# q and k laid out head dimension first by the host: attention and two expert layers on one Trainium2 core

## The chip, the cores and the metric

The kernel runs on one core of one Trainium2 chip. The metric is the device time of one launch in microseconds (us); the host's part, which lays out the inputs, is not in it. Everything is computed in fp32 up to the second expert layer, which multiplies fp16 halves of split fp32 values. In the profile PE is TensorE (PEld its weight loads), DVE VectorE, ACT ScalarE, POOL GpSimd and SP SyncE, whose queue issues the DMAs.

## What is computed

```python
# q, k, v: (4, 8, 576, 64) = batch, heads, tokens, head dimension
scores = (1 / 8) * q @ k.T + slope[h] * -|i - j|      # ALiBi
scores = where(0 <= i - j < 128, scores, -1e9)        # causal window of 128
attn   = exp(scores - max) / (sum + 1e-9)
x      = (attn @ v) as (2304, 512)                    # tokens x heads*dim
# first expert layer, soft: 8 experts of 4 slots
logits = x @ phi                                      # (2304, 32)
slots  = softmax over tokens(logits).T @ x            # (32, 512)
out_s  = relu(slots_e @ w1[e]) @ w2[e]                # per expert
x      = softmax over slots(logits) @ out_s
# second expert layer, dense: gate by 8 Sinkhorn rounds, P (2304, 8)
out    = sum over e of P[:, e] * (relu(x @ m1[e]) @ m2[e])   # 512 -> 1024 -> 512
```

## The kernel before

Attention works on 18 tiles of 128 rows. A tile t is one chunk c (64 tokens, nine of them) of the two images j of a pair; partitions 0 to 63 belong to one image and 64 to 127 to the other. A tile is done in two steps (s = 2t and 2t + 1) of four head pairs' halves: two pairs g, each with heads a = 0, 1. The loop over s at lines 475 to 526 is the order of work on every engine, written by hand; the instructions of an engine run in that order.

- `load_nat` (127) loads q and k by tokens, 64 tokens x 8 heads x 64 values in one DMA, in runs of 256 bytes; `load_v` (137) loads v by tokens, again in runs of 256 bytes.
- `emit_tr` (147) turns q and k on PE, so that the head dimension lies on the partitions (two heads on 128), and copies them from PSUM to `qT` and into the ring `kT` of four slots; slots 0 and 1 have second images behind the ring (line 158), so that three chunks are always adjacent.
- `emit_qk` (169) makes the scores of a step: 8 products of 64 x 64 with up to 192 columns, each in one quarter of PE's array.
- `emit_sm` (188) adds the bias from `rel_sb` and takes the negated maximum on DVE; `emit_exp` (209) makes the exponentials on ACT, with their sum as accumulator output; `emit_nm` (216) divides by that sum on DVE.
- `emit_pt` (224) turns the weights on PE (up to six 128 x 128 transposes a step), and ACT copies them to `ptt`.
- `emit_pv` (237) multiplies: v is the stationary operand (`lhsT`), the weights move (`rhs`), and the result has the head dimension on the partitions: head a gives the output half, image j the tile `xp[j]`. From the third chunk on 8 products have 128 rows and 8 have 64 (`steps`, 251 and 253); in the first chunk all 8 have 64, in the second all 8 have 128.
- `emit_xt` (268) copies that to `xT` (head dimension on partitions), and `emit_x` (273) turns it into `xn` (tokens on partitions). Every four tiles `group` (343) and at the end `group_end` (379) do the softmax over tokens and collect the slots' inputs; both need `xT` and `xn`.

All three PSUM pools are small: three buffers for the scores (`ps_s`), three for everything that is turned (`ps_t`), one for the products with v (`ps_x`). SP issues all loads in program order; at most eight are on their way, since each waits for the one eight before it. Beside q, k and v it loads a quarter of an expert's w1 in each step from s = 2 on (`pre`), w2 of expert 0 at s = 26 and 30, then, where attention's pools have been, w2 of experts 1 to 3. The first expert layer (`mm1`, 780) starts with w1 of expert 0; m2 and m1 of the second layer's first expert go over w1 of experts 0 and 1 once these are used (`order`, 734). The second expert layer (from 888) is a long row of fp16 products with three parts per operand pair.

Of the kernel before, what the change touches and what calls it, by code (L numbers as in the profile page):

```python
# [20 lines left out]
NPRE = 8  # L21


@with_exitstack
def tile_kernel(ctx: ExitStack, tc: tile.TileContext, q, k, v, phi, w1, w2, w_gate, m1, m2, rel, out):
    nc = tc.nc
    B, H, S, D = q.shape
    N, DM = out.shape
    E, _, F = w1.shape
    NS = phi.shape[1]  # L30
# [26 lines left out]
    def load_part(nm, e, pool, part, nparts):  # L57
        if part == 0 and pool is not None:
            wt[nm, e] = pool.tile([128, 4096], F32, tag="w", name="w")
        t = wt[nm, e]  # L60
        src = {"w1": w1, "w2": w2, "m1": m1, "m2": m2}[nm][e].rearrange("(c p) f -> p c f", p=128)
        n = src.shape[1]
        n0, n1 = n * part // nparts, n * (part + 1) // nparts
        nc.sync.dma_start(out=t.rearrange("p (c f) -> p c f", c=n)[:, n0:n1, :], in_=src[:, n0:n1, :])
# [30 lines left out]
    with tc.manual_schedule():  # L95
        with ExitStack() as ab:
# [5 lines left out]
            with ExitStack() as at:  # L102
                nat = at.enter_context(tc.tile_pool(name="nat", bufs=2))
                one = at.enter_context(tc.tile_pool(name="a1", bufs=1))
                ep = at.enter_context(tc.tile_pool(name="ep", bufs=3))
# [7 lines left out]

                kT = one.tile([128, 4, 2, 6 * CH], F32, name="kT")
# [3 lines left out]

                rel_sb = one.tile([128, 2, 4, 192], F32, name="rel_sb")


                qT = one.tile([128, 4, 2, 64], F32, name="qT")

                natt = {}
                vt = {}

                def load_nat(t):
                    bp, c = divmod(t, NCH)
                    for nm, src in (("k", k), ("q", q)):
                        nt_ = nat.tile([128, H, D], F32, tag=nm + "n", name=nm + "n")  # L130
                        for j in range(2):
                            nc.sync.dma_start(
                                out=nt_[CH * j:CH * j + CH],
                                in_=src[2 * bp + j, :, CH * c:CH * c + CH, :].rearrange("h i d -> i h d"))
                        natt[nm, t] = nt_

                def load_v(bp, c, j=None):


                    j = c % 2 if j is None else j  # L140
                    t = vp.tile([128, H, D], F32, tag="v%d" % j, name="v")
                    r0, r1 = 64 if c < 0 else 0, 64 if c == NCH - 1 else 128
                    s0 = max(CH * c, 0)
                    nc.sync.dma_start(out=t[r0:r1], in_=v[2 * bp + j].rearrange("h s d -> s h d")[s0:s0 + r1 - r0])
                    vt[bp, c, j] = t

                def emit_tr(t, nm, gs=range(4)):
                    src = natt[nm, t]
                    ps = ps_t.tile([128, 4, 128], F32, tag="pt", name="pt")
                    for i, g in enumerate(gs):  # L150
                        nc.tensor.transpose(
                            ps[:, i, :], src[:, 2 * g:2 * g + 2, :].rearrange("p a d -> p (a d)"), idn)
                    pv_ = ps[:, 0:len(gs), :].rearrange("p g (j i) -> p g j i", j=2)
                    if nm == "k":
                        sl_ = t % 4
                        nc.vector.tensor_copy(out=kT[:, :, :, CH * sl_:CH * sl_ + CH], in_=pv_)
                        if sl_ < 2 and t >= 4:
                            nc.scalar.copy(out=kT[:, :, :, CH * (sl_ + 4):CH * (sl_ + 5)], in_=pv_)
                    else:
                        nc.vector.tensor_copy(out=qT[:, gs[0]:gs[-1] + 1], in_=pv_)  # L160
# [8 lines left out]
                def emit_qk(s):  # L169
                    t, hf = divmod(s, 2)  # L170
                    c = t % NCH
                    nch = min(c, 2) + 1
                    k0 = CH * ((t - nch + 1) % 4)
                    k1 = k0 + CH * nch
                    col = 192 - (k1 - k0)

                    ps = [ps_s.tile([128, 2, 256], F32, tag="s", name="s") for _ in range(2)]
                    for gg in range(2):
                        g = 2 * hf + gg
                        for j in range(2):  # L180
                            for a in range(2):
                                r0, c0 = CH * (a ^ j), CH * a
                                nc.tensor.matmul(ps[j][c0:c0 + CH, gg, col:192], lhsT=qT[r0:r0 + CH, g, j, :],
                                                 rhs=kT[r0:r0 + CH, g, j, k0:k1], start=True, stop=True,
                                                 tile_position=(r0, c0))
                    sc[s] = (ps, col)

                def emit_sm(s):
# [6 lines left out]
                    sm = sp.tile([128, 4], F32, tag="sm", name="sm")  # L195
                    c = (s // 2) % NCH
                    for hh in range(4):
# [7 lines left out]
                            in1=rel_sb[:, j, 2 * hf + gg, col:192], scale=-0.125, scalar=3e38,  # L205
                            op0=ALU.add, op1=ALU.min, accum_out=mx[:, hh:hh + 1])
                    et[s] = (e_t, runs, sm, mx)

                def emit_exp(s):
                    _, runs, sm, mx = et[s]  # L210
                    for hh in range(4):
                        nc.scalar.activation(  # L212
                            out=runs[hh], in_=runs[hh], func=AF.Exp,
                            bias=mx[:, hh:hh + 1], scale=-1.0, accum_out=sm[:, hh:hh + 1])

                def emit_nm(s):
                    _, runs, sm, _ = et[s]
                    rc = sp.tile([128, 4], F32, tag="rc", name="rc")
                    nc.vector.tensor_scalar_add(rc, sm, 1e-9)
                    nc.vector.reciprocal(rc, rc)  # L220
                    for hh in range(4):
                        nc.vector.tensor_scalar_mul(runs[hh], runs[hh], rc[:, hh:hh + 1])

                def emit_pt(s):
                    c = (s // 2) % NCH
                    e_t, _, _, _ = et.pop(s)
# [10 lines left out]
                def emit_pv(s):  # L237
# [3 lines left out]
                    if hf == 0:  # L241
                        xps[t] = [ps_x.tile([128, 4, 64], F32, tag="xp%d" % j, name="xp") for j in range(2)]
                    xp = xps[t]
# [11 lines left out]

                    for i0 in range(0, len(steps), 2):
                        for gg in range(2):
                            g = 2 * hf + gg
                            for i in (i0, i0 + 1):
                                j, vc, r0, r1, blk = steps[i]  # L260
                                for a in range(2):
                                    o = 128 * blk + 64 * (a ^ j)
                                    nc.tensor.matmul(
                                        xp[j][64 * a:64 * a + 64, g, :],
                                        lhsT=vt[bp, vc, j][r0:r1, 2 * g + a, :], rhs=ptt[r0:r1, gg, o:o + 64],
                                        start=(i < 2 and gg == 0), stop=(i >= len(steps) - 2), skip_group_check=True)

                def emit_xt(t):
                    xT[t] = sp.tile([128, DC, 128], F32, tag="xT", name="xT", bufs=4)
                    for j, xp in enumerate(xps.pop(t)):  # L270
                        nc.vector.tensor_copy(out=xT[t][:, :, 64 * j:64 * j + 64], in_=xp)

                def emit_x(t):
                    ps = ps_t.tile([128, 4, 128], F32, tag="pt", name="pt")
                    for cc in range(DC):
                        nc.tensor.transpose(ps[:, cc, :], xT[t][:, cc, :], idn)
                    xn[t] = sp.tile([128, DM], F32, tag="xn", name="xn", bufs=4)
# [977 lines left out]
```

## Time and profile before

| | us |
|---|---|
| median of 3 runs | 965.99 (965.25 to 966.2) |
| profiled execution: span from first to last instruction | 962.0 |
| what lies around the span, by the median run | 4.0 |
| PE busy | 928.2 (96%) |
| DVE busy | 737.5 (77%) |
| ACT busy | 612.5 (64%) |
| POOL busy | 542.1 (56%) |

The shares are means over stages with different limits. Attention runs up to about 152 us, the first expert layer to 205, the second fills the rest. The page's slices of 24 us show a DMA share of 80% and more up to about 190 us and of 60% to 216, then little; of 94,659 DMA packets 63,696 are smaller than 512 bytes. PE and PEld overlap: a product's weights are loaded while others run, and products in different parts of the array overlap, so that an operation's mean duration times its count can be far above its busy time. Each fp32 product shows as two records, a transpose as one.

### The profile page before, as it was taken

What the parts mean: (1) busy time and instruction counts of PE and PEld (TensorE: products, weight loads), DVE (VectorE), ACT (ScalarE), POOL (GpSimd) and SP (SyncE); (2) the same over time, 40 slices, a digit from 0 to 9 for tenths busy, and PEclk for the clock granted to TensorE, in tenths of its full rate; (3) what the DMA queues carried; (4) which work ended last, traced back from release to release, by engine and by line L of the source; (5) the groups of instructions that cost most, each with busy time, mean ns of one, the idle gap of its engine ahead of it and who ended that gap; (6) DMA issues with size and microseconds to landing.
All of it is one profiled execution on the core that took longest, in us unless ns stands there. A gap on an engine that the chain in (4) does not pass through costs nothing.

```text
span 962.0 us, 24533 instructions
## 1 busy us (share of the span) xinstructions
PE 928.2 (96%) x9629; PEld 781.6 (81%) x9629; DVE 737.5 (77%) x1919; ACT 612.5 (64%) x1494; POOL 542.1 (56%) x624
## 2 busy tenths in 40 slices
PE   8898899889999999999999999999999999999997
PEld 5666675357888888888888888888888888888886
DVE  6888896666988777787778777877777778777775
ACT  5777784746767777666657664766576656764442
POOL 1000001213788479848974986589658956985442
PEclk9999999999999999999999999999999999999999
DMA  8999999960200500040022002200220020001222
GB/s 175 250 239 236 264 292 322 383 227 2 99 2 2 171 17 2 31 158 1 2 86 102 1 1 91 98 1 2 94 95 1 2 97 4 1 2 34 56 48 64
DMA packets 94659, 90.20 MB, mean 94 GB/s; under 512 B 63696, under 2 KB 67792, under 8 KB 94544
## 3 DMA queue, kind: packets, MB, share of 16 engines
q1 hardware_dynamic: 94544, 88.64, 32.0%
q8 instruction: 75, 1.23, 0.5%
q14 instruction: 40, 0.33, 0.1%
HBM read 82.07 MB, written 4.72 MB: 90 GB/s over the span
## 4 chain that ended last, share of the span: by engine, by line
PE 74%; DVE 2%; ACT 1%; issue 0%; DVEq 0%
PE x L1053 38%; PE y L1053 28%; PE z L979 6%; PE m L681 1%; DVE ops L992 0%; DVE s L1004 0%; PE m L556 0%; DVE acc L1065 0%; DVE prob L948 0%; ACT acc L1063 0%; ACT ops L989 0%; DVE rs L936 0%; ACT r L1000 0%; PE m L942 0%; ACT t L564 0%
## 5 line engine op out<-in xcount | busy, mean ns | idle before, releaser
L1053 PEld LDWEIGHTS <-ops 128*128 128x128 f16 x6048 | 592.2, 98 | 75.1 <-issue 5.0
L1011 POOL TENSOR_TENSOR ops<-s,ops 128x512 f16<-128x512 f32 x287 | 332.0, 1159 | 224.1 <-ACT ops L1008 223.7
L1053 PE MATMUL x<-w2h,ops 128*128 128x256 f16 x2304 | 413.8, 273 | 3.3 <-ACT acc L1063 2.7
L1053 PE MATMUL y<-w2h,ops 128*128 128x256 f16 x1728 | 319.0, 273 | 0.3 <-POOL ops L1011 0.2
L1053 PE MATMUL x<-w2l,ops 128*128 128x256 f16 x1152 | 314.1, 273 | 0.0
L1008 ACT CAST ops<-s 128x512 f16<-128x512 f32 x288 | 177.5, 617 | 212.7 <-DVE s L1004 210.3
L1053 PE MATMUL y<-w2l,ops 128*128 128x256 f16 x864 | 235.5, 273 | 0.0
L1067 DVE SCALAR_TENSOR_TENSOR acc<-x,pe,acc 128x256 f32<-128x256 f32 x252 | 121.7, 483 | 76.9 <-PE x L1053 75.5
L989 ACT ACTIVATE ops<-z 128x512 f16<-128x512 f32 x216 | 128.6, 595 | 35.1 <-PE z L979 33.4
L992 DVE SCALAR_TENSOR_TENSOR ops<-z,ops 128x512 f16<-128x512 f32 x216 | 146.9, 680 | 0.0
L1067 DVE SCALAR_TENSOR_TENSOR acc<-y,pe,acc 128x256 f32<-128x256 f32 x189 | 91.2, 483 | 58.5 <-PE y L1053 58.1
L639 POOL TENSOR_TENSOR w2l<-w,w2h 128x256 f16<-128x256 f32 x168 | 112.4, 673 | 0.0
L1004 DVE SCALAR_TENSOR_TENSOR s<-z,r 128x512 f32<-128x512 f32 x144 | 98.2, 682 | 12.0 <-ACT r L1000 6.0
L1004 DVE SCALAR_TENSOR_TENSOR s<-z,s 128x512 f32<-128x512 f32 x144 | 98.2, 682 | 6.3 <-ACT ops L989 5.3
L979 PE MATMUL z<-ct,stk 128*128 128x256 f16 x576 | 86.5, 273 | 1.4 <-ACT stk L724 0.7
L774 POOL MEMSET hz<- 128x480 f32 x2 | 1.0, 498 | 140.5 <-ACT fo L313 139.2
L642 ACT CAST w2h<-w 128x256 f16<-128x256 f32 x168 | 67.5, 402 | 0.4 <-POOL w L639 0.4
L979 PEld LDWEIGHTS <-stk 128*128 128x128 f16 x576 | 55.6, 98 | 10.8 <-issue 2.6
L212 ACT ACTIVATE et<-et,mx 128x192 f32<-128x192 f32 (+2 forms) x144 | 61.2, 430 | 3.6 <-DVE mx L203 3.6
L234 ACT COPY ptt<-pt 128x384 f32<-128x384 f32 (+2 forms) x72 | 30.1, 444 | 19.6 <-PE pt L233 19.3
L1000 ACT ACTIVATE r<-z 128x512 f32<-128x512 f32 x72 | 42.4, 589 | 0.0
L639 POOL TENSOR_TENSOR w<-w 128x256 f32<-128x256 f32 x56 | 41.0, 733 | 0.0
(192 smaller groups left out, 898.4 us busy)
## 6 DMA issues: line engine op xcount, KB each, us to landing
w<-in_moe_w_dram SPq DMA_DIRECT2D x68, 512.0 KB, 7.0
w<-in_moe_w_dram SPq DMA_DIRECT2D x14, 2048.0 KB, 8.3
kn<-in_k_dram SPq DMA_DIRECT2D x36, 128.0 KB, 5.6
qn<-in_q_dram SPq DMA_DIRECT2D x36, 128.0 KB, 5.5
v<-in_v_dram SPq DMA_DIRECT2D x18, 256.0 KB, 6.2
out_dram<-acc SPq DMA_DIRECT2D x34, 128.0 KB, 2.4
w<-in_moe_w_dram SPq DMA_DIRECT2D x2, 1024.0 KB, 6.9
stk<-sh SPq DMA_DIRECT2D x56, 16.0 KB, 1.8
```

The lines of the kernel that those rows point to most:

```text
L212: nc.scalar.activation(out=runs[hh], in_=runs[hh], func=AF.Exp, bias=mx[:, hh:hh + 1], scale=-1.0, accum_out=sm[:, hh:hh + 1])
L639: nc.gpsimd.tensor_tensor(out=out_, in0=x_, in1=y_, op=ALU.subtract)
L642: nc.scalar.copy(out=hi[:, i, r], in_=src[:, r])
L979: nc.tensor.matmul(ps[:, i], lhsT=stk[e][:, 128 * ft:128 * ft + 128], rhs=ct.rearrange("p (a n) t -> p a n t", a=2)[:, :, n, :], start=Tru ...
L989: nc.scalar.activation(out=ops_[m][:, k_, 0], in_=zb(m, i, j), func=AF.Relu)
L992: nc.vector.scalar_tensor_tensor(out=ops_[m][:, k_, 1], in0=zb(m, i, j), scalar=0.0, in1=ops_[m][:, k_, 0], op0=ALU.max, op1=ALU.subtract)
L1000: nc.scalar.activation(out=new_sum(m, "r21"), in_=zb(m, 2, 1), func=AF.Relu)
L1004: nc.vector.scalar_tensor_tensor(out=new_sum(m, nm), in0=zb(m, i, j), scalar=0.0, in1=o, op0=ALU.max, op1=op)
L1008: nc.scalar.copy(out=ops_[m][:, k_, 0], in_=sm_[m, nm])
L1011: eng.tensor_tensor(out=ops_[m][:, k_, 1], in0=sm_[m, nm], in1=ops_[m][:, k_, 0], op=ALU.subtract)
L1053: nc.tensor.matmul(out_, lhsT=a_[:, k_, l_, i, :], rhs=r_[:, k_, i, :], start=(first and j == 0), stop=(j == len(todo) - 1 and 1 in parts) ...
L1067: nc.vector.scalar_tensor_tensor(out=o, in0=ps, scalar=pe_[e][:, t:t + 1], in1=o, op0=ALU.mult, op1=ALU.add)
```

## The change

The host's `layouts` puts q and k head dimension first, chunk by chunk, as `qT` and `kT` want them; appends to each head of v two columns of ones (`DV` = 66, of which one is used); lays the expert weights out by partition, so that a partition's 4096 values are adjacent; and makes the four biases of `rel_sb` itself. In the kernel:

- `load_qk` loads q and k straight into `qT` (three buffers) and `kT` (a ring of `RK` = 6 slots without second images; where three chunks wrap, a score product becomes two). `emit_tr` and its copies are gone.
- `emit_exp` makes no sums and `emit_nm` is gone: weights stay unnormalised, and the ones column gives their sum.
- `emit_pv` has the weights as stationary operand and v with its ones as moving one: 66 columns, tokens on the partitions; image j gives the output half, and each step's half of the tile has a PSUM bank of its own. The same count of products.
- `emit_xn` divides as it copies from PSUM, two DVE products a tile, to `xn`; `emit_xt` turns `xn` into `xT` by four transposes.
- The pipeline is one step shorter (products at s - 2, transposes of the weights at s - 1, after the products), w2 of expert 0 loads at steps 33 and 35, v one step earlier, and the warm-up is 12 products in one piece.

On PE the order of two steps in the middle of attention was the following (`s` scores, `qn` and `kn` transposes of q and k, `et` of the weights, `xp` products with v, `xT` the tile turned back):

```order
L183 MATMUL s<-kT,qT 64x192 x8
L151 MATMUL pt<-idn,qn 128x128 x2
L233 MATMUL pt<-idn,et 128x128 x6
L151 MATMUL pt<-idn,kn 128x128 x4
L263 MATMUL xp<-ptt,v 64x64 x16
L183 MATMUL s<-kT,qT 64x192 x8
L151 MATMUL pt<-idn,qn 128x128 x2
L233 MATMUL pt<-idn,et 128x128 x6
L276 MATMUL pt<-idn,xT 128x128 x4
L263 MATMUL xp<-ptt,v 64x64 x16
```

and is now

```order
L157 MATMUL s<-kT,qT 64x192 x8
L228 MATMUL xp<-v,ptt 64x66 x16
L248 MATMUL pt<-idn,xn 128x128 x4
L199 MATMUL pt<-idn,et 128x128 x6
L157 MATMUL s<-kT,qT 64x192 x8
L228 MATMUL xp<-v,ptt 64x66 x16
L199 MATMUL pt<-idn,et 128x128 x6
```

The eight transposes of q and k per tile are gone, the products with v stand ahead of the transposes of the next step's weights, and the four transposes per tile take `xn` in place of `xT`. On SP's queue the loads of one tile in the middle of attention (`w` a quarter of an expert's w1) were

```order
L132 DMA kn<-in_k_dram 64x8x64 x2
L132 DMA qn<-in_q_dram 64x8x64 x2
L64 DMA w<-in_moe_w_dram 128x1024
L144 DMA v<-in_v_dram 128x8x64 x2
L64 DMA w<-in_moe_w_dram 128x1024
```

and are now

```order
L121 DMA kT<-in_k_dram 128x512
L123 DMA qT<-in_q_dram 128x512
L132 DMA v<-in_v_dram 128x528
L63 DMA w<-in_moe_w_dram 128x1024 x2
L121 DMA kT<-in_k_dram 128x512
```

Two loads of 64 tokens each for k and for q became one each of 128 partitions, and v comes in one load per tile, ahead of both quarters of w1. The core of the diff:

```diff
@@ loads
-        src = {"w1": w1, "w2": w2, "m1": m1, "m2": m2}[nm][e].rearrange("(c p) f -> p c f", p=128)
-        nc.sync.dma_start(out=t.rearrange("p (c f) -> p c f", c=n)[:, n0:n1, :], in_=src[:, n0:n1, :])
+        src = {"w1": w1, "w2": w2, "m1": m1, "m2": m2}[nm][e]
+        n0, n1 = 4096 * part // nparts, 4096 * (part + 1) // nparts
+        nc.sync.dma_start(out=t[:, n0:n1], in_=src[:, n0:n1])
...
+                kT = one.tile([128, RK, 4, 2, CH], F32, name="kT")
...
+                def load_qk(t):
+                    nc.sync.dma_start(out=kT[:, t % RK].rearrange("p g j i -> p (g j i)"), in_=k[t])
+                    qT[t] = qp.tile([128, 4, 2, CH], F32, tag="q", name="qT")
+                    nc.sync.dma_start(out=qT[t].rearrange("p g j i -> p (g j i)"), in_=q[t])
@@ scores
+                    first = (t - n + 1) % RK
+                    m = min(n, RK - first)
+                    runs = [(first, m, 0)] + ([(0, n - m, m)] if m < n else [])
...
+                                for sl_, w, o in runs:
+                                    k0 = col + CH * o
+                                    nc.tensor.matmul(
+                                        ps[j][c0:c0 + CH, gg, k0:k0 + CH * w].rearrange("p (n i) -> p n i", n=w),
+                                        lhsT=qT[t][r0:r0 + CH, g, j, :],
+                                        rhs=kT[r0:r0 + CH, sl_:sl_ + w, g, j, :], start=True, stop=True,
+                                        tile_position=(r0, c0))
@@ exponentials
-                            bias=mx[:, hh:hh + 1], scale=-1.0, accum_out=sm[:, hh:hh + 1])
-
-                def emit_nm(s):
...
+                            out=runs[hh], in_=runs[hh], func=AF.Exp, bias=mx[:, hh:hh + 1], scale=-1.0)
@@ products with v
-                        xps[t] = [ps_x.tile([128, 4, 64], F32, tag="xp%d" % j, name="xp") for j in range(2)]
+                        xps[t] = ps_x.tile([128, 2, 512], F32, tag="xp", name="xp")
+                    xp = xps[t][:, hf, 0:4 * DV].rearrange("p (h d) -> p h d", h=4)
...
-                                for a in range(2):
-                                    o = 128 * blk + 64 * (a ^ j)
+                            for a in range(2):
+                                for i in (i0, i0 + 1):
+                                    j, vc, r0, r1, blk = steps[i]
+                                    o = 128 * blk + 64 * a
                                     nc.tensor.matmul(
-                                        xp[j][64 * a:64 * a + 64, g, :],
-                                        lhsT=vt[bp, vc, j][r0:r1, 2 * g + a, :], rhs=ptt[r0:r1, gg, o:o + 64],
-                                        start=(i < 2 and gg == 0), stop=(i >= len(steps) - 2), skip_group_check=True)
+                                        xp[CH * j:CH * j + CH, 2 * gg + a, :],
+                                        lhsT=ptt[r0:r1, gg, o:o + 64], rhs=vt[bp, vc, j][r0:r1, 4 * hf + 2 * gg + a, :],
+                                        start=(j not in begun), stop=(i >= len(steps) - 2), skip_group_check=True)
+                                    begun.add(j)
+
+                def emit_xn(t):
+                    xp = xps.pop(t)[:, :, 0:4 * DV].rearrange("p f (h d) -> p f h d", h=4)
+                    rc = sp.tile([128, 2, 4], F32, tag="rc", name="rc")
+                    nc.vector.tensor_scalar_add(rc, xp[:, :, :, D], 1e-9)
+                    nc.vector.reciprocal(rc, rc)
...
+                    for f in range(2):
+                        nc.vector.tensor_tensor(out=o[:, f], in0=xp[:, f, :, 0:D],
+                                                in1=rc[:, f].to_broadcast([128, 4, D]), op=ALU.mult)
 
                 def emit_xt(t):
...
+                        nc.tensor.transpose(ps[:, cc, :], xn[t][:, 128 * cc:128 * cc + 128], idn)
+                    nc.vector.tensor_copy(out=xT[t], in_=ps)
@@ the loop over steps
+                        if hf == 0 and t + 2 < NT:
+                            load_qk(t + 2)
...
+                        if s in (NST - 3, NST - 1):
+                            load_w2_0(*((0, 4) if s == NST - 3 else (4, FC)))
                         emit_qk(s)
+                        emit_sm(s)
+                        emit_exp(s)
+                    if 2 <= s and s - 2 < NST:
+                        emit_pv(s - 2)
+                        if s % 2 == 1:
+                            emit_xn((s - 2) // 2)
+                            px.append((s + 1, (s - 2) // 2))
+                    turned()
                     if 1 <= s and s - 1 < NST:
+                        emit_pt(s - 1)
```

## Rows read from the trace of the kernel before

**Rows 1.** Stretches: us; busy PE, PEld, DVE, ACT, POOL; clock; DMA share; GB/s.

```profile
8.27:34.08 25.81, 21.04 (x286) 14.21 (x290) 21.72 (x121) 17.24 (x75) 1.39 (x3) 0.93 1.01 221
34.08:140.46 106.38, 96.56 (x1680) 70.16 (x1674) 95.27 (x477) 82.56 (x304) 0.00 (x0) 1.00 1.09 254
140.46:159.22 18.76, 17.02 (x268) 11.96 (x258) 12.81 (x55) 9.47 (x35) 1.34 (x4) 1.00 1.01 364
159.22:204.68 45.46, 39.52 (x482) 18.48 (x483) 30.66 (x102) 24.63 (x73) 8.19 (x12) 1.00 0.90 327
204.68:962.00 757.32, 747.49 (x6912) 660.63 (x6911) 575.20 (x1162) 476.13 (x1006) 528.87 (x596) 1.00 0.14 46
```

**Rows 2.** Timeline of PE, one step: start us, us, instructions merged [idle before].

```profile
113.65 0.88 PE L183 MATMUL s<-kT,qT 64*64 64x192 f32 x16
114.46 0.44 PE L151 MATMUL pt<-idn,qn 128*128 128x128 f32 x2
114.73 0.82 PE L233 MATMUL pt<-idn,et 128*128 128x128 f32 x6
115.42 0.66 PE L151 MATMUL pt<-idn,kn 128*128 128x128 f32 x4
116.00 1.08 PE L263 MATMUL xp<-ptt,v 128*64 128x64 f32 x32
```

**Rows 3.** Waits of PE in the first stretch: us in total, times, longest.

```profile
PE pt L151 <- DMA kn<-in_k_dram: 2.5, 2, 1.7
```

**Rows 4.** Waits of PE in the second stretch.

```profile
PE pt L233 <- DVE cn L332: 3.6, 3, 1.3
PE pt L233 <- ACT kT L158: 2.7, 5, 0.9
...
PE pt L151 <- DVE mx L203: 0.8, 1, 0.8
```

**Rows 5.** Table by stretches, line 263 alone: us; PE busy, PEld busy (records).

```profile
116.00:116.62 0.62, 0.62 (x17) 0.55 (x17) 1.00 0.97 311
116.62:117.01 0.39, 0.39 (x20) 0.32 (x16) 1.00 0.95 305
```

**Rows 6.** PE instructions by form, 0 to 160 us: busy, mean ns, idle before.

```profile
L183 PE MATMUL s<-kT,qT 64*64 64x192 f32 x448 | 26.0, 337 | 1.1 <-issue 1.1
```

**Rows 7.** Groups of DVE instructions by line, 0 to 300 us.

```profile
L203 DVE CUSTOM_DVE_ANT_0 et<-s,rel_sb 128x192 f32<-128x192 f32 (+2 forms) x144 | 39.3, 329 | 0.3 <-PE s L183 0.3
L222 DVE TENSOR_SCALAR et<-et,rc 128x192 f32<-128x192 f32 (+2 forms) x144 | 34.7, 305 | 1.3
...
L156 DVE COPY kT<-pt 128x512 f32<-128x512 f32 x18 | 12.3, 686 | 5.3 <-PE pt L151 5.3
...
L1065 DVE TENSOR_TENSOR acc<-y,acc 128x256 f32<-128x256 f32 x23 | 9.6, 418 | 3.4 <-PE y L1053 3.3
```

**Rows 8.** Groups of ACT instructions by form, 0 to 160 us.

```profile
L212 ACT ACTIVATE et<-et,mx 128x192 f32<-128x192 f32 x112 | 49.6, 448 | 0.7 <-DVE mx L203 0.7
L212 ACT ACTIVATION_READ_ACCUMULATOR et<-et,mx 128x1 f32 x144 | 27.5, 191 | 0.0
L234 ACT COPY ptt<-pt 128x384 f32<-128x384 f32 x56 | 25.4, 480 | 15.5 <-PE pt L233 15.3
```

**Rows 9.** Table by stretches: with 256-byte pieces queued, and with w2's alone.

```profile
70.00:100.00 30.00, 26.89 (x466) 19.04 (x465) 27.19 (x147) 23.12 (x93) 0.00 (x0) 1.00 1.12 234
149.50:155.50 6.00, 5.09 (x69) 3.15 (x71) 3.17 (x14) 2.18 (x7) 0.88 (x4) 1.00 1.05 386
```

**Rows 10.** Timeline of SP's queue: issues after the first w1 product.

```profile
159.92 15.66 SPq L64 DMA_DIRECT2D w<-in_moe_w_dram  x16
```

**Rows 11.** Timeline of PE: warm-up; first m1 product; first z of the second layer.

```profile
1.36 3.79 PE L83 MATMUL warm<-idn 128*128 128x128 f32 x16 [1.36 <-POOL idn masks.py:199]
...
198.34 1.93 PE L681 MATMUL m<-w,st 128*32 128x256 f32 x32
...
204.68 0.49 PE L979 MATMUL z<-ct,stk 128*128 128x256 f16 x3 [0.71 <-ACT stk L724]
```

More of the change, by code (lines that the diff above doesn't have):

```diff
@@ L26, in tile_kernel @@
     nc = tc.nc
-    B, H, S, D = q.shape
+    B, S, H, D, E, F, NS = 4, 576, 8, 64, 8, 1024, 32
     N, DM = out.shape
-    E, _, F = w1.shape
-    NS = phi.shape[1]
     CH = 64
@@ L122, in tile_kernel @@
-                qT = one.tile([128, 4, 2, 64], F32, name="qT")
-                natt = {}
+                qT = {}
                 vt = {}
[L127 to L135, printed above, removed]
+                def load_qk(t):
+                    nc.sync.dma_start(out=kT[:, t % RK].rearrange("p g j i -> p (g j i)"), in_=k[t])
+                    qT[t] = qp.tile([128, 4, 2, CH], F32, tag="q", name="qT")
+                    nc.sync.dma_start(out=qT[t].rearrange("p g j i -> p (g j i)"), in_=q[t])
@@ L145, in load_v @@
                     vt[bp, c, j] = t
[L147 to L160, printed above, removed]
@@ L268, in emit_xt @@
                 def emit_xt(t):
[L269 to L273, printed above, removed]
                     ps = ps_t.tile([128, 4, 128], F32, tag="pt", name="pt")
                     for cc in range(DC):
-                        nc.tensor.transpose(ps[:, cc, :], xT[t][:, cc, :], idn)
-                    xn[t] = sp.tile([128, DM], F32, tag="xn", name="xn", bufs=4)
-                    nc.scalar.copy(out=xn[t], in_=ps.rearrange("p a b -> p (a b)"))
+                        nc.tensor.transpose(ps[:, cc, :], xn[t][:, 128 * cc:128 * cc + 128], idn)
@@ L1227, in alibi, with layouts, heads, rows @@
     rel = 128 + p % 64 - np.arange(192)[None, :]
-    return np.where((rel >= 0) & (rel < window), rel / (1 + p // 64), 1e12).astype(np.float32)
+    rel = np.where((rel >= 0) & (rel < window), rel / (1 + p // 64), 1e12).astype(np.float32)
+    return np.stack([-(2.0 ** (2 - 2 * g)) * rel for g in range(4)], 1).astype(np.float32).reshape(128, 768)
+def layouts(inputs):
+    import numpy as np
+    def heads(x):
+        x = x.reshape(2, 2, 4, 2, 9, 64, 64)
+        x = np.stack([x[:, 0], x[:, 1][:, :, ::-1]], 1)
+        return x.transpose(0, 4, 3, 6, 2, 1, 5).reshape(18, 128, 512)
+    def rows(w):
+        e, n, m = w.shape
+        return w.reshape(e, n // 128, 128, m).transpose(0, 2, 1, 3).reshape(e, 128, n // 128 * m)
+    v = inputs["v"].transpose(0, 2, 1, 3)
+    out = {"q": heads(inputs["q"]), "k": heads(inputs["k"]),
+           "v": np.concatenate([v, np.ones(v.shape[:3] + (DV - 64,), v.dtype)], 3).reshape(4, 576, 8 * DV)}
+    for nm in ("moe_phi", "moe2_w_gate"):
+        out[nm] = rows(inputs[nm][None])[0]
+    for nm in ("moe_w1", "moe_w2", "moe2_w1", "moe2_w2"):
+        out[nm] = rows(inputs[nm])
+    out["alibi"] = alibi()
+    return out
 def kernel(**inputs):
```

136 lines of the change are left out of this document (42 added, 94 removed).

## The prediction

> **What bounds the kernel now.** I read the table by stretches first [rows 1]. Its five stretches are the first eight steps of attention, the other 27 up to the last scores, the tail up to the first product with w1 of the first expert layer, the rest of that layer, and the second expert layer. In the second stretch four resources are nearly full at once: PE is busy 96.56 of 106.38 us, DVE 95.27, ACT 82.56, and the DMA share is 1.09 at 254 GB/s. In the last stretch PE is busy 747 of 757 us and the change adds or takes nothing there, so those 757 us stay. Then one step of attention on PE [rows 2]: scores, two transposes of q, six of the weights, four of k (every second step), the products with v, without a gap from 113.65 to 117.01. The mean over the 27 steps is 106.38/27 = 3.94 us. So PE's own work sets most of a step, and the waits [rows 4] the rest. A part taken off PE is time; a part taken off DVE or ACT counts only as far as PE waited for it.
>
> **PE: what goes.** A tile has two pairs of q transposes (114.46 to 114.73, 0.27 us each) and one set of k (115.42 to 116.00, 0.58) [rows 2]: 1.13 us. 17 tiles do this after the first scores: 4 in the first stretch (4.5 us), 13 in the second (14.7 us).
>
> **PE: what comes.** The products with v change sides. Before, a step with 16 of them starts with 8 of 128 rows, 0.62 us, then come 8 of 64 rows, 0.39 [rows 5]. That smaller products run side by side in parts of the array the scores show: 448 records of 337 ns fit in 26.0 us, about six at once [rows 6]. The 128-row products have two column halves to run in, the 64-row ones four quarters, so the first half takes twice as many rounds as the second; with the same change of shape c ahead of each, 8r + c = 0.62 and 4r + c = 0.39 give a round of r = 0.058 us. Now the image (j) fixes the output half and, in the 64-row steps, the row half with it, so two quarters are left and those products take 8 rounds, too: +0.23 us in each step but those of a second chunk, 32 of 36: 4 in the first stretch, 25 in the second, 3 in the tail: +0.9, +5.8, +0.7. Bounds: nothing, if these rounds are bound by issue, and +0.39 a step. 66 columns for 64 are 3% of a round, under 0.5 us in all.
>
> The ring of six slots makes the scores wrap in 8 steps, 16 products instead of 8. The columns are the same, so the lower bound is nothing; if each second product holds up the next quarter, a step's 0.81 us (113.65 to 114.46) doubles: +6.5 us. The quarters overlap so freely [rows 6] that I take +0.2 a step, 1.6 us.
>
> **DVE and ACT.** DVE loses 34.7 us of normalising and 12.3 of kT copies [rows 7], the qT copies too. It gains two normalising products a tile, nearest the 418 ns row with a 256-column PSUM operand [rows 7]: 36 x 0.42 = 15 us; one 512-column copy replaces two of half the size. ACT loses 27.5 us of accumulator reads [rows 8] and the copies of xn and of the ring's second image. None of this is on PE's path by itself; it shortens waits. Of the second stretch's waits [rows 4] those for kT and mx, 3.5 us, go with their transposes. The largest, 3.6 us for cn, is a PSUM buffer that the group's softmax holds until DVE comes to it; with over 30 us less on DVE I take half away, 1.8. Together -5.3; bounds -3.5 and -9.8, all of PE's idle time there [rows 1].
>
> The exponentials now stand ahead of the copies of the previous step's transposes on ACT, so the next products wait for both. An exponential has a pitch of 49.6/112 = 0.44 us with its 0.19 us read [rows 8]; without the read I take 0.35 (bounds 0.25 and 0.44). From the start of the scores that is 0.81 + a row minimum of 0.30 (39.3/144 and some) [rows 7] + 4 x 0.35 + 2 x 0.45 [rows 8] = 3.4 us, and PE comes to those products 3.5 to 4.1 us after it. So I charge nothing, but see the third rival.
>
> **DMA.** q, k and v come in 256-byte pieces now, afterwards in 2 KB and 2.1 KB. The rows: 234 GB/s while such pieces are queued, 386 when only w2's pieces of 2 KB are [rows 9]. Two steps then need 0.5 MB of q and k, 0.27 of v and 1.05 of w1, 1.8 MB: 4.7 us at 386 GB/s against some 6.9 us of PE. So DMA drops out as a bound there. In the first stretch the 2.5 us of waits for k [rows 3] go, and the clock with them: 0.93 granted over 25.81 us [rows 1] is 1.8 us lost, one drop to 1.2 GHz behind the 1.7 us wait. Nothing that I see takes the wait's place: by step 6 3.4 MB must have landed, 9 us at 386 GB/s, and step 6 of eight starts late in a stretch that runs from 7.0 to some 25.
>
> At the end w2_0 moves from steps 26 and 30 to 33 and 35, past the last w1 parts on SP. From step 33 to the first w1 product 8.9 MB must go, 23 us at 386 GB/s; the time there is two steps of 3.5 and the tail of 17.3, 24. The load that goes over w1 waits for that product anyway (issued 159.92) [rows 10], so I charge nothing: bounds 0 and +3 us, by which m2_0 would come late to ACT.
>
> **The sum.** Start: 8 warm-up products took 3.79 us [rows 11]; 12, with no other work ahead of the scores, end near 7.0 instead of the 8.27 at which the scores start: -1.3. First stretch: -4.5 -2.5 -1.8 +0.9; the pipeline is one step shorter, so one step's products and transposes (1.6 us) move in from the tail; of the other 2.3 us of idle time (25.81 - 21.04 - 2.5) I take half away: -7.4. Second: -14.7 +5.8 +1.6 -5.3 = -12.6. Tail: -1.6 +0.7 -0.6 (one set of transposes moves ahead of the group's end) = -1.5. First expert layer: 0. Sum -22.8. Against the profiled execution: 962.0 - 22.8 = 939.2 us of span. The runs' median, 966.0, is 4.0 longer than this span, which I take as what lies around it: 943.
>
> **Rivals.**
> 1. *The weights' loads set the pace, slower than before.* The new layout makes each quarter of w1 128 pieces of 4 KB, 16 KB apart, instead of one closed block of 512 KB. Were that to run at the 234 GB/s of the mixed stage [rows 9], the 52.5 MB up to the second layer's first m1 (14.3 of q, k, v, 33.6 of w1 and w2, 4.2 of m2 and m1, 0.4 of biases) would take 224 us. The product with that m1 is at 198.34 now, the second layer's start 6.3 later [rows 11], so the layer would start at 231 instead of 204.7: 992 us. It decides from 52.5 MB/198.3 us = 265 GB/s down. For: the trace of before has no load of this shape. Against: pieces of 2 KB at 386. The Trainium skill, "DMA: Bandwidth & Descriptors" (Latency and other measured facts), measured copies at 207 GB/s with the partitions' rows 512 KiB apart and 103 with 4 MiB; at 16 KiB no run here shows it. Chance 0.06.
> 2. *The products with v run one after the other.* Two row halves now write one PSUM tile in the 64-row products. If they exclude each other, 16 rounds take the place of 8: 32 x 0.46 = 15 us more, 958. Against: in the scores two row halves write one tile already, with six records at once [rows 6]. The Trainium skill, "TensorEngine Tiling (Array Packing)" (Gotcha 1: PSUM Pressure), says that different row tiles cannot access the same PSUM bank at the same time; by it the sum would be this 958, and as far as the scores go the trace disagrees. Chance 0.07.
> 3. *A new wait takes part of it.* There is one buffer for a tile's products, free only after four DVE instructions (two short ones of some 0.2 and 2 x 0.42, 1.2 us); PE has 0.69 of transposes and 0.81 of scores for cover. If DVE comes to them behind four row minima, 1.2 us, PE waits up to 0.9 us a tile, and exponentials at their old pitch cost some 4 x 0.09 a step: a third of 18 x 0.9 + 36 x 0.36 = 29 us is 10 us less gain, 953. For: both chains are tight. Against: DVE has a quarter of its time free. Chance 0.13.
> 4. *No change*: the first layer's loads take back what attention gains, 966. Against: the load after the first w1 product waits for that product [rows 10]. Chance 0.02.
>
> **Chances and range.** The forecast has 0.72, its own range 932 to 950: all idle time gone and no loss in the products (-11) against the wrap and the expert layer at their dear ends (+7). 0.2% is 2 us, about what a measurement tells from no change. Faster: 0.72 + 0.07 + 0.13 = 0.92; same 0.02; slower 0.06. The range for 8 in 10 takes in the third rival: 931 to 954.
>
> **What would show it.** Right: the second stretch 93 to 94 us with DVE busy under 78% and PE over 93%; no wait for DMA before the first w1 product; the 64-row products at 0.6 us a step; the second layer as long as before to within 1 us. Wrong: a DMA share near 1 through attention at less than 300 GB/s (first rival), products of over 1.6 us a step (second), DVE's normalising or ACT's copies at the head of PE's waits with over 6 us (third).

## The result and the profile after

The changed kernel takes **936.59 us** (median of 4 runs, 936.04 to 941.53) against 965.62 (963.68 to 966.2) for the kernel before on the same chip: ratio 0.9711, 95% interval 0.968 to 0.9741. That is faster, inside the range of 931 to 954, and 6.4 us under the forecast of 943.0. The profiled execution spans 934.3 us.

The same five stretches as in [rows 1], now of the changed kernel (us; busy PE, PEld, DVE, ACT, POOL; clock; DMA share; GB/s):

```profile
6.45:23.85 17.40, 16.05 (x295) 12.28 (x294) 11.93 (x77) 13.74 (x45) 0.00 (x0) 1.00 0.95 335
23.85:114.53 90.68, 87.55 (x1725) 69.49 (x1724) 62.83 (x319) 63.23 (x179) 0.00 (x0) 1.00 0.83 298
114.53:131.89 17.36, 14.39 (x185) 10.03 (x181) 10.28 (x42) 5.43 (x18) 1.23 (x4) 1.00 0.89 333
131.89:177.33 45.44, 39.52 (x481) 18.49 (x482) 30.64 (x102) 24.61 (x73) 8.08 (x12) 1.00 0.91 341
177.33:934.30 756.97, 746.06 (x6912) 659.40 (x6911) 576.02 (x1162) 475.90 (x1006) 528.81 (x596) 1.00 0.14 46
```

All of the gain but 0.4 us lies ahead of the first product with w1: start -1.8, first eight steps -8.4, the 27 steps -15.7, tail -1.4. The two expert layers are as long as before. In the 27 steps PE is busy 97% of the time where it was 91%, DVE 69% where it was 90%; the DMA share fell from 1.09 to 0.83 while the rate rose from 254 to 298 GB/s.

One step on PE, as in [rows 2] (start us, us, merged instructions):

```profile
103.90 0.88 PE L157 MATMUL s<-kT,qT 64*64 64x192 f32 x16
104.71 1.30 PE L228 MATMUL xp<-v,ptt 128*64 128x66 f32 x32
105.95 0.66 PE L248 MATMUL pt<-idn,xn 128*128 128x128 f32 x4
106.44 0.82 PE L199 MATMUL pt<-idn,et 128*128 128x128 f32 x6
107.19 0.39 PE L157 MATMUL s<-kT,qT 64*64 64x192 f32 x4
```

From start to start the products with v take 1.24 us (104.71 to 105.95), 1.01 before. The transposes of q and k are gone, and nothing waits in this step. What PE still waits for in the first two stretches (us in total, times, longest), to set beside [rows 3] and [rows 4]:

```profile
PE pt L290 <- ACT ptt L200: 1.5, 3, 1.1
PE xp L228 <- DVE xn L242: 1.0, 3, 0.5
PE s L157 <- DVE mx L178: 0.5, 1, 0.5
```

No wait for DMA is left there, and none for cn or kT.

### The profile page after: what moved, and what is told of

Read it like the earlier page. It is cut to its first block, busy times and chain, and to the rows that moved or that the text cites. A ratio compares the mean times of both kernels' runs of the same rounds, so it can differ in the third digit from the quotient of the medians.

```text
span 934.3 us, 24029 instructions
## 1 busy us (share of the span) xinstructions
PE 908.7 (97%) x9615; PEld 774.7 (83%) x9615; DVE 692.5 (74%) x1703; ACT 584.2 (63%) x1320; POOL 539.1 (58%) x620
## 4 chain that ended last, share of the span: by engine, by line
PE 76%; DVE 2%; ACT 1%; issue 0%; DVEq 0%
PE x L1000 39%; PE y L1000 29%; PE z L926 6%; PE m L628 1%; DVE ops L939 0%; DVE s L951 0%; PE m L503 0%; DVE acc L1012 0%; DVE prob L895 0%; ACT acc L1010 0%; ACT ops L936 0%; DVE rs L883 0%; ACT r L947 0%; PE m L889 0%; ACT t L511 0%
## 5 line engine op out<-in xcount | busy, mean ns | idle before, releaser
L187 ACT ACTIVATE et<-et,mx 128x192 f32<-128x192 f32 (+2 forms) x144 | 51.1, 426 | 28.1 <-DVE mx L178 28.0
L178 DVE CUSTOM_DVE_ANT_0 et<-s,rel_sb 128x192 f32<-128x192 f32 (+2 forms) x144 | 39.7, 331 | 25.0 <-PE s L157 22.7
L228 PEld LDWEIGHTS xp<-v,ptt 64*64 64x64 f32 (+1 forms) x1024 | 35.4, 135 | 12.2 <-ACT ptt L200 7.9
L228 PE MATMUL xp<-v,ptt 64*64 64x66 f32 (+1 forms) x1024 | 42.2, 226 | 2.3 <-DVE xn L242 1.0
```

The costliest lines, as they stand in the source:

```text
L187: nc.scalar.activation(out=runs[hh], in_=runs[hh], func=AF.Exp, bias=mx[:, hh:hh + 1], scale=-1.0)
L228: nc.tensor.matmul(xp[CH * j:CH * j + CH, 2 * gg + a, :], lhsT=ptt[r0:r1, gg, o:o + 64], rhs=vt[bp, vc, j][r0:r1, 4 * hf + 2 * gg + a, :], ...
```

## The experiments

Two questions: which part of the change carries the gain (PE's transposes, DVE and ACT, or the loads), and why the sum was 5 us short. Ratios are to the kernel before, run on the same chip; by that measure the changed kernel stands at 0.9711.

**One part at a time, on the kernel before.**

*q and k head dimension first* (b_qk):

```diff
-                load_nat(0)
+                load_qk(0)
...
-                            emit_tr(t1 + 1, "q", range(2 * hf1, 2 * hf1 + 2))
...
-                            emit_tr(t + 1, "k")
...
```

> The kernel before with only q and k laid out head dimension first (no transposes of q and k, ring of six slots with wrapped scores); weights still normalised ahead of their transposes, products with v as before. If PE's own work is what counts: 17 x 1.13 us of transposes go (-19), the waits for k (2.5), for the copies of k and for mx (3.5), and the slow clock (1.8), +0.7 for the wraps: about -25 us, 941 us, most of the whole change. If relief of DVE and ACT is what counts: DVE still normalises 34.7 us and ACT still reads 27.5 us of sums, so the steps stay near the 3.9 us that DVE and ACT allow: less than half of the change, 952 to 960 us, with PE idle 10% or more from the ninth step on.

Measured: 938.35 us, ratio 0.9728 (0.971 to 0.9745). Its first eight steps and its 27:

```profile
6.18:23.93 17.75, 14.41 (x258) 10.31 (x260) 16.27 (x108) 16.04 (x75) 1.70 (x4) 1.00 1.08 296
23.93:115.17 91.24, 84.81 (x1701) 64.07 (x1696) 78.92 (x440) 76.29 (x296) 0.00 (x0) 0.98 0.95 305
```

This part alone is nearly the whole change, though DVE still normalises (78.92 us busy) and ACT still reads its sums (76.29).

*The values' part* (b_pv; the bias table, too, is laid out as in the change, which makes room for the tiles):

```diff
-                            emit_xt(t3)
-
-                            px.append((s + 3 * (t3 % 4 == 0), t3))
+                            emit_xn(t3)
+                            px.append((s + 1, t3))
...
-                        emit_nm(s - 1)
...
```

> The kernel before with only the values' part: ones column, products with tokens as rows, normalising from PSUM, one transpose set per tile after it; q and k still transposed on PE. If PE's own work is what counts: +0.23 us in 32 steps, +7.4, against shorter waits (the wait for cn 3.6 and a part of the rest): between -3 and +6 us, 963 to 972 us. If relief of DVE and ACT is what counts: most of the 29 us, 945 us or less.

Measured: 963.98 us, ratio 0.9991 (0.9975 to 1.0007). Its 27 steps, and PE's longest waits there:

```profile
32.68:138.00 105.32, 99.26 (x1675) 76.00 (x1673) 77.32 (x357) 64.44 (x183) 0.00 (x0) 1.00 1.10 261
```
```profile
PE pt L224 <- DVE cn L329: 2.1, 3, 1.0
PE pt L151 <- DMA kn<-in_k_dram: 1.5, 1, 1.5
PE pt L151 <- DVE mx L202: 1.4, 2, 1.0
```

Against [rows 1], 18 us less on DVE and 18 less on ACT shorten the 27 steps by 1.1 us, net of PE's own work, which is 2.7 us more. The tail is 3.5 us longer (22.22 us against 18.76, with a wait of 1.4 us for cn), so this part just pays for its own costs. One thing limits the reading: the small pieces of q and k are still loaded (share 1.10, 1.5 us of waits for k), so how much the relief would give with fast loads isn't seen here. The ratios bound it: from b_qk, where q and k come in large pieces, to the whole change it is 0.2% (0.9728 to 0.9711), within the intervals.

*The weights' layout* (b_w):

```diff
-        src = {"w1": w1, "w2": w2, "m1": m1, "m2": m2}[nm][e].rearrange("(c p) f -> p c f", p=128)
...
+        src = {"w1": w1, "w2": w2, "m1": m1, "m2": m2}[nm][e]
...
```

> The kernel before with only the expert weights laid out by partition. If the loads of weights never set the pace, before or after: 965.6 us as before, within 1 us, attention 8.27 to 159.2 us and the second layer 757 us as before. If pieces of one partition 16 KB apart are slow (first rival): up to 992 us. If the new layout alone speeds up the first expert layer: 2 to 5 us faster, all of it between 159 and 205 us.

Measured: 966.68 us, ratio 1.0023 (1.0004 to 1.0043). Its first stretch and its two expert layers, and PE's longest wait in that first stretch:

```profile
7.92:33.63 25.71, 19.55 (x286) 13.33 (x290) 21.64 (x121) 17.33 (x76) 1.60 (x4) 1.00 1.05 219
...
161.49:206.93 45.44, 39.53 (x481) 18.50 (x482) 30.63 (x102) 24.62 (x73) 8.16 (x12) 1.00 0.89 330
206.93:964.50 757.57, 747.53 (x6912) 660.69 (x6911) 576.03 (x1162) 476.17 (x1006) 528.86 (x596) 1.00 0.14 46
```
```profile
28.77 0.63 PE L148 MATMUL pt<-idn,kn 128*128 128x128 f32 x4 [2.73 <-DMA kn<-in_k_dram]
```

The first rival falls: both expert layers are as long as before (45.44 and 757.57 us). In the profile PE waits 6.1 us for k's loads during attention, 2.5 before; that is where a loss of 0.2% can lie, but one trace doesn't settle so little.

The three ratios add up to -2.6%, the whole change is -2.9%. The rest, within the intervals, is left for the new order of the steps, the longer warm-up and what the parts do to each other; none of these was tried alone on the kernel before.

**The size of the pieces.** b_qk takes away transposes and small pieces together. Two runs part them. *Large pieces, transposes kept* (b_big, on the kernel before):

```diff
-                                out=nt_[CH * j:CH * j + CH],
-                                in_=src[2 * bp + j, :, CH * c:CH * c + CH, :].rearrange("h i d -> i h d"))
+                                out=nt_[CH * j:CH * j + CH].rearrange("p h d -> p (h d)"),
+                                in_=src[2 * bp + j, CH * c:CH * c + CH])
...
```

> The kernel before with q, k and v stored by rows of 512, so that their loads move pieces of 2 KB, and everything on the engines as before: q and k are still transposed on PE. If the transposes on PE are what the change removes: only the waits for k and the slow clock behind them go, 2.5 + 1.8 us, 960 to 962 us. If the small pieces held the attention stage back: also what the small pieces cost the changed kernel (9.2 us in the 27 steps, 3.3 in the first eight), so 950 to 953 us.

*Small pieces, no transposes* (a_256, on the changed kernel):

```diff
-                    nc.sync.dma_start(out=kT[:, t % RK].rearrange("p g j i -> p (g j i)"), in_=k[t])
+                    nc.sync.dma_start(out=kT[:, t % RK].rearrange("p g j i -> p (g j) i"), in_=k[t].rearrange("x p i -> p x i"))
...
```

> The changed kernel with q, k and v stored so that their loads again move pieces of 256 bytes (264 for v); all else as in the change. If the size of pieces is not what the change lives on (PE sets the step, DMA has room): 936.6 to 940 us. If it is: the stretch of the 27 steps moves 27.0 MB in 90.7 us now; at the 254 GB/s of that stretch before it takes 106 us, so about 950 us, with waits of PE for DMA in the first steps.

Measured: b_big 959.24 us, ratio 0.9951 (0.9935 to 0.9968); a_256 949.39 us, ratio 0.985 (0.9828 to 0.9872). The 27 steps of b_big, then of a_256, and what PE waits for there in a_256:

```profile
31.28:135.74 104.46, 96.26 (x1679) 70.06 (x1674) 94.75 (x475) 82.19 (x302) 0.00 (x0) 1.00 0.85 262
```
```profile
27.51:127.42 99.91, 91.20 (x1726) 72.29 (x1725) 62.99 (x319) 63.54 (x179) 0.00 (x0) 0.97 1.05 266
```
```profile
PE s L157 <- DMA qT<-in_q_dram: 3.9, 2, 3.2
PE xp L228 <- issue: 1.7, 3, 1.1
...
PE xp L228 <- DMA v<-in_v_dram: 1.0, 1, 1.0
```

With the transposes on PE, large pieces are worth 0.5%, 4.7 us, and the DMA share falls to 0.85 almost for nothing. Without the transposes, small pieces cost 1.4% (0.985 against 0.9711), some 13 us: at 266 GB/s and a share of 1.05 PE waits 4.9 us for q and v, which the changed kernel doesn't, and its own work takes 3.7 us longer (91.20 us against 87.55) at a clock of 0.97; the first stretch, too, is longer, 20.74 us at a clock of 0.84. Over the whole execution all four runs of a_256 have a lower clock, 0.988 to 0.990, than those of the changed kernel, 0.994 to 0.998. So the whole change with small pieces is worth 1.5%, large pieces with the transposes 0.5%, and both 2.9%. The two parts of the layout need each other; neither worth is a constant that could be added.

**ACT's reads put back** (a_acc):

```diff
-                            out=runs[hh], in_=runs[hh], func=AF.Exp, bias=mx[:, hh:hh + 1], scale=-1.0)
+                            out=runs[hh], in_=runs[hh], func=AF.Exp, bias=mx[:, hh:hh + 1], scale=-1.0,
+                            accum_out=sm[s][:, hh:hh + 1])
...
```

> The changed kernel with the exponentials' sums still read (the sums are not used): ACT gets 144 reads of 0.19 us, 27.5 us, back. If ACT's room covers them (63 of 91 us busy in the 27 steps): 936.6 to 938 us. If the chain scores, minima, exponentials, copies is tight (0.81 + 0.3 + 4 x 0.37 + 2 x 0.47 = 3.5 us now, 4.3 with the reads, against 3.66 to 4.1 us until PE comes to the products): 0.2 to 0.6 us in each of 34 steps, 943 to 957 us.

Measured: 941.41 us (938.88 to 947.8), ratio 0.9778 (0.9739 to 0.9817). In the profile it is 2.8 us longer than the changed kernel, and PE waits for the copies before the products. Below are that wait, the 27 steps, and one step on ACT, from the first exponential to the copies, here and in the changed kernel:

```profile
PE xp L231 <- ACT ptt L203: 2.5, 6, 0.7
```
```profile
24.97:117.17 92.20, 88.81 (x1725) 69.96 (x1724) 62.94 (x319) 72.54 (x289) 0.00 (x0) 1.00 0.82 294
```
```profile
101.44 0.46 ACT L189 ACTIVATE et<-et,mx 128x192 f32<-128x192 f32 x1 [1.09 <-DVE mx L180]
101.80 0.19 ACT L189 ACTIVATION_READ_ACCUMULATOR et<-et,mx 128x1 f32 x1
101.90 0.44 ACT L189 ACTIVATE et<-et,mx 128x192 f32<-128x192 f32 x1
...
103.21 0.83 ACT L203 COPY ptt<-pt 128x384 f32<-128x384 f32 x2
```
```profile
102.44 1.50 ACT L187 ACTIVATE et<-et,mx 128x192 f32<-128x192 f32 x4 [0.70 <-DVE mx L178]
103.85 0.83 ACT L200 COPY ptt<-pt 128x384 f32<-128x384 f32 x2
```

The expectation had the reads too dear. Part of a read lies over the next exponential: four exponentials take 1.77 us with reads and 1.41 without, 0.36 us a step and not 4 x 0.19. In the 27 steps ACT's busy time rises by 9.3 us (72.54 against 63.23), over attention by 12, not by 27.5. Even so PE comes to wait, 0.7 us in the 27 steps and the rest in the first steps and the tail, so the chain is nearly due. How much time it costs is not settled, as the interval just overlaps with that of the change. The third rival's mechanism is real at the old pitch; at the new one this wait for the copies is gone from the list, and of the rival's other half, the wait for `xn`, 1.0 us is left.

**All four quarters for the 64-row products** (a_swapb): for every second pair of heads the two images trade places, in the weights and in v's layout, the pairs write two PSUM banks, and the 64-row products alternate between the pairs.

```diff
-                        o = 384 * gg + w * ((j + c) % 2)
+                        o = 384 * gg + w * ((j + gg + c) % 2)
...
-                                    j, vc, r0, r1, blk = steps[i]
+                                    x, vc, r0, r1, blk = steps[i]
+                                    j = x ^ gg
...
-                                        xp[CH * j:CH * j + CH, 2 * gg + a, :],
+                                        xp[CH * j:CH * j + CH, gg, 2 * hf + a, :],
...
```

> The changed kernel with the two images trading places for every second pair of heads, and the pairs' products in two PSUM banks: the 64-row products can then use all four quarters of the array, two row halves writing the same 64 output partitions in different banks. If the 64-row products are held back only by having two of four quarters: 4 rounds in place of 8, -0.23 us in each of 32 steps, 929 us, and the products of a step at 1.0 us. If row halves that write the same output partitions exclude each other: 936.6 us, 1.24 us a step. If the chain over DVE and ACT comes due first: 931 to 935 us with new waits of PE for copies of ACT.

Measured: 935.36 us, ratio 0.9703 (0.9684 to 0.9722), not to be told from the change. One step, the first two stretches, and a wait in the first:

```profile
104.68 0.88 PE L157 MATMUL s<-kT,qT 64*64 64x192 f32 x16
105.49 1.08 PE L231 MATMUL xp<-v,ptt 128*64 128x66 f32 x32
106.50 0.66 PE L252 MATMUL pt<-idn,xn 128*128 128x128 f32 x4
```
```profile
6.77:27.16 20.39, 18.19 (x295) 13.73 (x295) 11.72 (x77) 13.69 (x44) 0.00 (x0) 0.83 0.87 283
27.16:114.69 87.53, 83.08 (x1726) 64.30 (x1725) 62.41 (x319) 63.20 (x179) 0.00 (x0) 1.00 0.86 313
```
```profile
PE s L157 <- DVE mx L178: 1.4, 1, 1.4
```

The products take 1.01 us (105.49 to 106.50): the +0.23 was the missing quarters, and row halves that write the same output partitions in two banks do run together. Both in one bank was not tried. The 27 steps gain 3.2 us, not 25 x 0.23 = 5.8; PE's idle time grew by 1.3. And the first stretch lost 3 us: its clock is 0.83, behind a wait of 1.4 us for minima. Those waited for the bias table, which took 6.6 us to land in this execution and 3.5 in the changed kernel's.

**The start.** *8 warm-up products in place of 12* (a_warm8):

```diff
-                warm(ps_t, "pt", idn, 12)
+                warm(ps_t, "pt", idn, 8)
```

> The changed kernel with 8 warm-up products in place of 12. If the warm-up sets the start: the scores start 4 x 0.42 = 1.7 us earlier, at 4.8, 935 us. If the loads of the first k and q set it: no change, scores at 6.4 us. If the clock of the first scores falls for want of the work ahead: the first steps are slower and the gain is given back.

Measured: 940.7 us, ratio 0.9762 (0.9744 to 0.978). Its first stretch and four us of it, and the wait ahead of them:

```profile
4.90:25.20 20.30, 17.18 (x296) 13.42 (x295) 11.85 (x77) 13.79 (x45) 0.00 (x0) 0.92 0.94 327
...
8.00:12.00 4.00, 3.71 (x52) 2.92 (x52) 1.43 (x16) 2.90 (x13) 0.00 (x0) 0.57 1.05 363
```
```profile
PE s L157 <- DVE mx L178: 2.0, 1, 2.0
```

The scores start 1.5 us earlier and then wait 2.0 us for minima, which wait for the bias table; the clock behind that is 0.57 over the next four us, so mostly at its lower level, 1.2 GHz. Part of that wait is not the warm-up's doing: in this execution the table took 5.1 us to land, in the changed kernel's 3.5. As far as the four runs go (939.58 to 942.3), the longer warm-up of the change is cover for the loads.

*The table's loads* (a_late, then a_rel; the table is 384 KB in one load now, 192 KB in three before):

```diff
-                nc.sync.dma_start(out=rel_sb.rearrange("p g w -> p (g w)"), in_=rel)
                 load_qk(1)
+                nc.sync.dma_start(out=rel_sb.rearrange("p g w -> p (g w)"), in_=rel)
```
```diff
-                nc.sync.dma_start(out=rel_sb.rearrange("p g w -> p (g w)"), in_=rel)
+                rel_ = rel.rearrange("p (g w) -> p g w", g=4)
+                nc.sync.dma_start(out=rel_sb[:, :, 128:192], in_=rel_[:, :, 128:192])
+                nc.sync.dma_start(out=rel_sb[:, :, 0:128], in_=rel_[:, :, 0:128])
```

> The changed kernel with the bias table loaded behind k and q of the second tile, so some 1.3 us later (512 KB at about 390 GB/s). If a wait of the minima for this table early in attention is followed by the half clock: first stretch 20 to 21 us, granted clock under 0.9 in it, 939.5 to 941 us. If the wait costs only itself: 1.3 us, 937.5 us.

> The changed kernel with the bias table loaded in two parts, the 128 KB that the first tile's minima need ahead of the other 256 KB. If the wait for that table and the clock that falls behind it are what spreads the starts (first stretch 17.4 us at clock 1.00 in the changed kernel, 20.3 us where the table landed 1.6 to 3.1 us later): every run near 935.5 to 936.5 us and the first stretch at most 17.4 us. If the table has nothing to do with it: still some runs 3 to 5 us longer.

Measured: a_late 939.58 us, ratio 0.9727 (0.9703 to 0.9751), first stretch 19.42 us at clock 0.91 behind a wait of 1.4 us. a_rel 939.55 us (936.58 to 941.14), ratio 0.9719 (0.9694 to 0.9744). By the ratios neither can be told from the change; what they show is in the profiles. The first comes near its theory, a little milder (forecast: 20 to 21 us at under 0.9). The second doesn't follow its own: its first stretch keeps the full clock but takes 18.5 us, not the 17.4 expected, runs still spread, and in the profiled one the clock falls elsewhere, in the tail and behind it:

```profile
115.13:134.17 19.04, 16.17 (x184) 11.57 (x181) 10.29 (x42) 5.44 (x18) 1.23 (x4) 0.89 0.88 330
134.17:179.84 45.67, 40.58 (x481) 18.81 (x482) 30.82 (x102) 24.62 (x73) 8.09 (x12) 0.97 0.88 329
```

So the table's wait is one place of the drop and not the only one.

**Together** (a_best: a_swapb and a_rel; a_best_dve: also the second copy of a step's weights on DVE):

```diff
-                        nc.scalar.copy(out=ptt[:, gg, 0:128 * n], in_=ps[:, 0:n, :].rearrange("p a b -> p (a b)"))
+                        copy = nc.scalar.copy if gg == 0 else nc.vector.tensor_copy
+                        copy(out=ptt[:, gg, 0:128 * n], in_=ps[:, 0:n, :].rearrange("p a b -> p (a b)"))
```

> The changed kernel with the images trading places for every second pair of heads (a_swapb) and the bias table in two parts (a_rel). If the table's wait hid what a_swapb gained: start and first stretch as in the changed kernel or 0.9 us better, second stretch 87.5 us as in a_swapb, so 931 to 932.5 us. If not: 934 to 936 us.

> As a_best, with the second of the two copies of transposed weights in each step made by DVE in place of ACT (36 copies of 0.47 us). If the chain over ACT is what keeps PE waiting now: 1 to 3 us under a_best. If DVE's own order holds it (the copy stands behind four minima and the normalising there): as a_best or up to 4 us slower.

Measured: a_best 934.47 us (932.73 to 936.11), ratio 0.967 (0.9645 to 0.9694): under the change's 0.9711, with intervals that overlap, so a gain of some 4 us is not shown; it is the second of its two forecasts that came. Its 27 steps took 90.67 us in the profiled execution, and part of that is again a drop of the clock:

```profile
68.00:91.00 23.00, 21.88 (x443) 16.85 (x443) 15.84 (x82) 15.08 (x43) 0.00 (x0) 0.93 0.95 349
```

a_best_dve 938.94 us, ratio 0.9718 (0.9692 to 0.9745): slower than a_best, by intervals that just touch. The wait moves to DVE, where normalising now stands behind the copies:

```profile
PE xp L232 <- DVE xn L246: 3.5, 6, 0.8
```

## Why the prediction was right, and where it was short

**What bounds the kernel.** Right: PE's own work. b_qk and b_pv show it from both sides. a_256 adds the condition: with the transposes gone it holds only while the loads come in large pieces. Of the prediction's signs of being right one was missed, a second stretch of 93 to 94 us (90.68); the others came.

**The sum**, -22.8 us of span, came out at -27.7. By its steps:

- *Start, -1.3*: -1.8. Twelve warm-up products ended at 6.45, not 7.0.
- *First stretch, -7.4*: -8.4. No drop of the clock, no wait for k. PE's idle time fell by 3.4 us, from 4.8 to 1.4, a little less than the 2.5 and the "half" of 2.3 in the sum. What was under-sized is PE's own work, which fell by 5.0 us (21.04 to 16.05) where the terms make 3.8; the transposes of q and k alone had taken 5.5 us there, not 4.5. But this is what differs between executions: the stretch takes 20.3 us where the clock falls (a_swapb, a_warm8).
- *Second, -12.6*: -15.7, the largest miss. The term for the waits, "-5.3; bounds -3.5 and -9.8", was under-sized: idle time fell from 9.8 to 3.1 us, -6.7. All 3.6 us for cn went, where I took half; the 1.5 us for ACT's copies are new. The term for the wraps was over-sized: "+0.2 a step" is +0.08, a wrapped step's scores in this row run 0.89 us to the next start for 0.81:

```profile
79.16 0.96 PE L157 MATMUL s<-kT,qT 64*64 64x128 f32 x32
80.05 1.30 PE L228 MATMUL xp<-v,ptt 128*64 128x66 f32 x32
```

  That is 0.7 us for 8 steps in place of 1.6. The 0.8 us still missing is what is left of larger misses, counted in the two traces from start to start with the waits left out: the transposes of q and k gave 15.5 us (14.7 in the sum), the products with v cost 7.3 (5.8), the transposes of the weights took 2.3 less (nothing in the sum), and the logits of one more group of tiles fall into this stretch, 1.0 more (nothing in the sum). That they nearly cancel is luck.
- *Products with v, +0.23 a step*: exact in the step shown, 1.24 for 1.01, and a_swapb shows the reason; over the stretch it is 0.29 on the mean of 25 steps (the 7.3 above). The second rival falls with it: both row halves of the 64-row products write one bank, in its two halves of partitions, and don't take turns. In a step of the first chunk all 8 products have 64 rows, and they take 0.61 us:

```profile
9.43 0.69 PE L228 MATMUL xp<-v,ptt 64*64 64x66 f32 x16
10.04 0.44 PE L199 MATMUL pt<-idn,et 128*128 128x128 f32 x2
```

  The Trainium skill, "TensorEngine Tiling (Array Packing)" (Gotcha 1: PSUM Pressure), says that different row tiles cannot access the same PSUM bank at the same time. Had they taken turns, a step's products would by my estimate have taken 1.7 us (1.24 and the rival's 0.46); the trace disagrees with 1.24. The price of 66 columns for 64, "under 0.5 us in all", was added up wrongly (3% of 16 rounds of 0.058 us in 36 steps is 1.0 us), but the 1.24 shows no such cost.
- *Tail, -1.5*: -1.4. *First expert layer, 0*: 0.0; the late loads of w2_0 delay nothing. *Second layer*: -0.35, and the clock differs there: its first 5.3 us had a clock of 0.68 before and 1.00 after.
- *Around the span, +4.0*: the failed step outside the sum. In all four runs of the changed kernel the time is 1.7 or 1.8 us above the core's span. I took the runs' median minus the span of one profiled execution for a constant; 2 us of it was that execution being one of the quicker ones.

**DMA.** "So DMA drops out as a bound there" is right (share 0.83), and the sum had only 4.3 us for it, the waits and the clock behind them. b_big puts that at 4.7. What the sum could not show is that these pieces would have cost 13 us once PE was faster.

**ACT.** "I charge nothing" for the exponentials ahead of the copies holds with the reads gone; a_acc shows how near it was. Its pitch of 0.35 us without the read is what the trace shows (1.41 us for four). "ACT loses 27.5 us of accumulator reads" is more than twice the 12 us that they cost in a_acc, as a read lies partly over the next exponential; the sum didn't use it.

## What to carry to other kernels

Price a part by the engine that ends the step: 18 us off DVE and 18 off ACT, with 2.7 more on PE, gave 1 us in the 27 steps, while q's and k's transposes off PE together with small pieces off the loads gave nearly all. Then ask of each resource that was hidden whether it still is at the new pace: the small pieces cost 5 us before the transposes went and 13 after, so that without large pieces about half of the gain would have been left. And take what lies around a span from executions that have both numbers.

## What was not expected of the hardware

- Two row halves of the array that write the same 64 output partitions in two PSUM banks run side by side: 16 products (32 records) in 1.01 us against 1.24.
- In a_warm8, a_swapb and a_late a wait of 1.4 to 2.0 us on PE in the first steps was followed by microseconds at the lower clock (0.57 between 8 and 12 us in a_warm8), which by the clock of the first stretch cost another 1.6 to 3.5 us. But the wait alone doesn't decide it: in b_w PE waited 2.7 us for k and kept the full clock, in a_256 the clock fell in the first stretch without a wait of PE over 0.6 us, and in a_rel the drop came in the tail (0.89). What decides stays open; it is 2 to 5 us of spread in a kernel whose attention stage is otherwise at PE's pace.
